# Earlier first operands for a TensorE-bound kernel: other input loads, filler transposes, merged last stores and a new order table

## The chip, the cores and the metric

The kernel runs on one core of one Trainium2 chip. The metric is the device time of one execution in microseconds, the median of several runs. The core has five engines that are named as in the profile: PE (TensorE, matrix products; PEld is its weight load), DVE (VectorE), ACT (ScalarE), POOL (GpSimd) and SP (SyncE, which here only issues transfers). They run at the same time, each through its own instructions in order, and wait for one another by semaphores. Data moves between the off-chip memory and the on-chip memory by DMA transfers, which SP, ACT and POOL issue. POOL's transfers can convert fp32 to fp16 on the way; those of SP and ACT here move bytes as they are.

## The reference

Two stages. The first is an attention between tokens and a small state, for 8 batches and 8 heads, with 512 tokens, 32 state rows and 64 columns per head:

```
scores  = scale * x @ state^T ;  a  = softmax(scores)  ; xread = a  @ state
scores2 = scale * state @ x^T ;  a2 = softmax(scores2) ; sread = a2 @ x
tokens  = concat([xread, sread])          # 8 * 544 = 4352 tokens of 512 columns
```

The second is a mixture of 8 experts over these tokens, with weights P from a gate that is normalised 8 times over rows and columns:

```
P = exp(tokens @ w_gate - max) ; 8 times: P /= row sums, P /= column sums, P *= N / E
out = sum over e of  P[:, e] * ( relu(tokens @ w1[e]) @ w2[e] )      # 512 -> 1024 -> 512
```

## The kernel before

**Two programs behind each other.** The second one, from about 140 us to the end, is a plain loop over experts 1 to 7 and over 9 blocks of tokens (8 blocks of 512, and the 256 `sread` tokens). It is dense on PE: `hidden_ps` (L255) for the first product, seven half-size products per block in `layer2` (L334) for the second, and DVE's scaled additions into `acc` (L348). It ends with `layer2_last`: expert 7 on the 256 `sread` tokens, two rows of 128 tokens, matrix products at L312, scaled additions at L314 and the last stores at L317. Row 0 is one product of 512 columns, row 1 two of 256. Each row is stored in four transfers of 32 partitions, alternately from SP and ACT.

**The first program** does all of the attention, expert 0, the gate and the start of expert 1. Its pieces of work are 736 numbered `ops`, and the text table `PLAN` lists them in the order in which they are issued, with the engine that gets each ("62P" is op 62 on PE). `issue` walks through this table. Each engine works in order, so the table fixes what stands ahead of what on PE, DVE, ACT, POOL and on SP's and ACT's transfer queues. The times beside the ops in the code are the planner's estimates that made the table; they do not act at run time.

**What the start consists of**, with the line by which the profile shows each:

- `state` is loaded by two transfers, from SP and ACT (L441), in pieces of 64 floats, and copied as fp16 to `st_in` (`place`: L419 when ACT copies, L421 when DVE does). PE transposes it in 16 products (`turn`, L492) and ACT or DVE copies the result to `stT` (`keep`).
- `x` of a batch (here x0, x1 and so on) is loaded in two halves of four heads by POOL (L468), with conversion to fp16. For x0 and x1 PE transposes each half in 8 products (`turnX`, L578), and two copies take them to `xT`. From x2 on, SP's transposing transfers do that (L591).
- Half a batch is a unit (u0 and u1 belong to x0, u2 and u3 to x1). Its scores are computed as state by tokens (`score`, L605, tile `psB`); u0 and u1 also as tokens by state (`scoreA`, L684, tile `psA`, with the spread-out copy `stD` of the state, cleared at L504). DVE takes maxima (L640, L688) and differences (L691), ACT exponentials (L652, L656), DVE sums and normalises (L666 to L670), PE transposes back (`turnA`, L709), and a copy makes `aT` (`keepA`).
- Expert 0's `w1` and `w2` come in four halves by POOL (L545, L548). `V` is the state times `w1` (L870), so that the first layer (`hidden_mul`, L897, tile `hps`) is V by `aT`. The second layer is L935. The gate uses `G` (L520), the state times `w_gate`.

Loads that POOL issues stand in one queue with POOL's normalisations (L662, L670). The first products at L897 need both units of x0, and with them PE's dense work begins.

Of the kernel before, what the change touches and what calls it, by code (L numbers as in the profile page):

```python
# [16 lines left out]
6G 0S 1S 2V 7H 44V 3A 33V 32A 34A 8G 56P 36P 35V 55H 37V 10H 45V 57A 42P 58V 9G 38P 40P 43A 59P 4S 39A 41V 5V  # L17
46V 62P 50H 51G 61A 71V 63P 60A 52G 64V 11G 72V 73A 80P 65V 12G 435P 401P 66A 81V 13H 79P 14G 82V 436A 88V
437A 404P 83A 67V 402A 137H 403A 89V 96H 97P 100P 84V 406A 68V 90A 98A 15G 85V 69P 86P 53G 405A 99V 87V 70A
103P 101A 102A 91V 409P 16H 92G 413P 104V 407P 410A 411P 105V 111A 438P 120P 414V 408A 419P 421P 106V 415P  # L20
112V 138S 121V 74V 439A 412A 422V 113V 417P 107A 54G 440A 75G 122V 432P 429P 123V 370V 420A 469P 128A 418A
416A 17G 108V 140P 124A 125V 423P 426P 471A 433P 114A 148V 93S 129V 430P 149V 172H 424P 76S 434A 115V 470A
109G 130V 139S 110V 126G 141V 131A 427P 18G 127V 142V 428V 431A 445P 143V 132V 94P 150A 95V 77P 425A 156P 116G
447P 151V 133V 78V 449P 446A 443P 441P 144A 455P 164V 152G 448A 117S 19H 450V 157V 444A 165V 173S 442A 451P
456A 166A 134S 20G 452A 453P 463P 158V 472P 207H 145V 175P 159V 183V 184V 457P 31G 146G 454A 176V 473A 160A
464P 185A 174S 460P 458P 461P 465A 147V 161V 21G 153S 177V 191P 47P 162G 474A 118P 167V 459A 154P 462A 178V
163V 135P 49A 168G 199V 22H 48V 179A 466P 136A 352P 475P 200V 192V 201A 193V 119V 467P 476A 194V 23G 195A 485P
202V 208S 210P 180V 169S 155A 218V 356P 353A 481P 357V 468A 487P 219V 24G 489P 181G 186V 211V 242H 486A 482A
477P 490V 488A 483P 479P 220A 170P 478A 503P 187G 480A 484V 171A 203G 196V 537P 209S 25H 212V 226P 197G 504A
505A 506P 213V 500P 182V 198V 26G 234V 221V 507A 222V 204S 188S 491P 27G 538A 227V 539A 501P 497P 502A 508A  # L30
492P 235V 243S 228V 244S 214A 229V 511P 215V 236A 523P 230A 498P 494P 216G 245P 495P 515P 512V 499A 277H 231V
524A 493A 517P 246V 253V 223S 496A 247V 521P 516A 237V 254V 519P 509P 522V 518A 248V 513P 232G 189P 520A 255A
205P 510V 224P 514V 540P 28H 278S 261P 249A 190V 269V 29G 225A 270V 262V 531P 534P 206V 238G 250V 532P 256V
358P 271A 535P 217V 541A 533A 233V 542A 312H 279S 263V 272V 536A 354P 280P 528P 543P 529P 525P 288V 289V 251G
555P 264V 281V 265A 282V 239S 257V 526P 359A 266V 544A 530V 556A 545P 355A 547P 549P 273G 553P 527A 546V 571P
313S 290A 548A 283V 605P 550A 554V 296P 267G 606V 304V 572A 305V 240P 573A 557P 284A 607A 558A 551P 297V 552A
568P 360P 258S 241V 285V 30G 291V 306A 559P 562P 574P 298V 252V 315P 299V 286V 569P 576A 268V 323V 563P 575A
274S 300A 560P 570A 292G 316V 361A 561A 581P 564A 307V 565P 362P 324V 317V 301V 325A 302G 566P 363V 582A 326V
579P 587P 583P 287V 314S 588V 591P 567A 580A 639P 608P 584A 592A 347H 303V 331P 577P 348G 641V 640A 610A 609A
339V 293S 589P 585P 275P 332V 259P 578A 327G 586A 260A 590A 294P 340V 308G 333V 341A 593P 309S 318V 319A 334V  # L40
295V 364P 594P 276V 328S 625P 619P 342V 595A 335A 365A 599P 320V 602P 343V 336V 600P 337V 603P 626A 321G 322V
329P 310P 350G 344S 601A 349G 311A 620V 345P 338V 346V 604V 366P 596P 330A 368P 369V 351G 597P 367A 371V 611P
372P 598A 695H 615P 617P 373V 612V 374P 375V 613P 614V 616A 623P 618A 621P 696H 711H 376A 705P 377V 642P 624A
622A 706A 707A 630P 643V 697V 708P 644A 378P 379V 631P 710A 627P 698V 380V 647P 632A 709A 636P 628P 381P 633P
699V 648V 637P 382V 634P 657P 629A 638A 383V 700V 653P 658A 655P 384P 651P 635A 701V 654A 725P 385V 723P 386V
702V 656A 726A 716P 652A 724A 717A 645P 659P 649P 714P 646A 650A 660A 387P 721P 715A 712P 727P 687P 722A 388V
728A 688A 667P 713A 664P 389V 390P 703V 665P 668P 391V 673P 674A 392V 661P 670P 669A 729V 393P 671P 394V 666A
662P 672A 677P 395V 718P 663A 678A 679P 675P 683P 719A 681P 720V 680A 676A 685P 396P 684A 682A 397V 686A 692P
704V 689P 693P 690P 730P 398V 694A 399P 733P 731V 691A 732A 735A 734A 400V
""".split()  # L50
ENGINES = {"P": "PE", "V": "DVE", "A": "ACT", "G": "POOL", "D": "DMA", "S": "SPQ", "H": "HOST"}
NT_ = 2
ETX = 0
POOLB = 1
# [50 lines left out]
def issue(ops):  # L105
    for step in PLAN:
        op = ops[int(step[:-1])]
        assert all(d.end for d in op.after) and ENGINES[step[-1]] in op.on
        for slot in op.takes:
            slot.ring.taken.append(slot)  # L110
            slot.tile = slot.make()
        op.emit(ENGINES[step[-1]])
        op.end = True
    assert all(op.end for op in ops) and len(PLAN) == len(ops)
# [3 lines left out]
def kernel(  # L118
# [9 lines left out]
    nc = tc.nc  # L128
# [170 lines left out]
    def layer2_last():  # L299
# [5 lines left out]
        for row in range(tn // 128):  # L305
# [10 lines left out]
            for i in range(nb):  # L316
                (nc.scalar if i % 2 else nc.sync).dma_start(  # L317
                    out=outs[row * nb + i], in_=acc[ds(i * Ns, Ns), k, :])
# [116 lines left out]
    st_in = spl.tile([128, B, NQ, 2, D], FP16, name="st_in")  # L435
    st_st = spl.tile([128, B, NQ, D], FP32, name="st_st")
    loads = []
    for g in range(2):
        def load(g=g):
            bs = ds(g * B // 2, B // 2)  # L440
            (nc.scalar if g else nc.sync).dma_start(  # L441
                out=st_st[:, bs], in_=state[bs].rearrange("b (q h) n d -> (h n) b q d", q=NQ))

        loads.append(dma((0, 0), 1.0, load, lands=2.7))
        ops[-1].since, ops[-1].hard = 0.5, 1
# [5 lines left out]
    wgd = dma((0, 2), 0.1, lambda: nc.sync.dma_start(  # L451
        out=wg_st, in_=moe_w_gate.rearrange("(kc p) e -> p kc e", p=128)))
    wgc = op((15.0,), {"DVE": (0.15, 0.25)}, lambda _: nc.vector.tensor_copy(out=wgh, in_=wg_st), [wgd])
    wgc.since = 20.0
# [7 lines left out]
    for b in range(B):  # L462
        x_ready.append([])
        part("x%d" % b)
        got = op((0, 1 + 2 * b), {"HOST": (0.0, 0.0)}, lambda _: None, takes=[xn[b]])
        for g in range(2):
            def load(b=b, g=g):
                nc.gpsimd.dma_start(  # L468
                    out=xn[b].tile[:, ds(g * 4, 4), :],
                    in_=x[b, ds(g * 4, 4), :, :].rearrange("h (p sc) d -> p h (sc d)", sc=NSC))  # L470

            x_ready[b].append(dma((0, 1 + 2 * b, g), 1.28 if b else 2.3 - 0.6 * g, load, [got], [], [xn[b]], "POOL"))
            ops[-1].since, ops[-1].hard = 0.7, 1
# [4 lines left out]
    bd = []  # L478
    for g in range(2):
        for s_ in range(2):  # L480
            def place(eng, g=g, s_=s_):
                bs = ds(g * B // 2, B // 2)
                copy(eng, st_in[:, bs, :, s_, :], st_st[:, bs])

            bd.append(op((0, 0, g), {"DVE": (0.50, 0.64)} if s_ else {"ACT": (0.50, 0.65)}, place, loads[g:g + 1] + warmed))
    stT_ready = []
    for g in range(4):
        ps = psum([128, 4, 128], FP16, "stT_ps")

        def turn(_, g=g, ps=ps):  # L490
            for i in range(4):
                nc.tensor.transpose(ps.tile[:, i], st_in[:, 2 * g + i // 2, i % 2].rearrange("p s d -> p (s d)"),  # L492
                                    identh)

        def keep(eng, g=g, ps=ps):
            copy(eng, stT[:, ds(2 * g, 2)].rearrange("p b q c -> p (b q) c"), ps.tile)

        t = op((0, 1, g), {"PE": (0.35, 0.55)}, turn, bd[g // 2 * 2:g // 2 * 2 + 2] + [makeh], [ps])
        stT_ready.append(op((0, 1, g), EVICT16, keep, [t], uses=[ps]))
    ND = (TOK + 1) // 2  # L500
    stD_ready = {}
    if TOK:
        stD = spl.tile([128, ND, NQ, 4, 2, Ns], FP16, name="stD")
        zd = op((0, 0, 0), {"POOL": (0.40, 0.50), "DVE": (0.25, 0.35)}, lambda eng: engines[eng].memset(stD, 0.0))  # L504
        for b in range(ND):
            def spread(eng, s_, b=b):
# [4 lines left out]
                               lambda eng, s_=s_, spread=spread: spread(eng, s_), stT_ready[b // 2:b // 2 + 1] + [zd])  # L511
# [55 lines left out]
    for b in range(B):  # L567
# [4 lines left out]
                  [x_ready[b][0]], [xT])  # L572
        for g in range(2 if b < NT else 0):
# [11 lines left out]
            t = op((due_x(2 * b + g) - 2.0, 0), {"PE": (0.70, 0.88)}, turnX, [x_ready[b][g], makeh], [ps], [xn[b]])  # L585
# [3 lines left out]
        for g in range(0 if b < NT else 2):  # L589
# [5 lines left out]
            xt_ready.append([dma((due_x(2 * b - 2), 0, g), 2.0, turn, [x_ready[b][g], gotT], [], [xn[b], xT], lands=0.8)])  # L595
            ops[-1].moves, ops[-1].xbar = (3.0, 0.8), 1
            ops[-1].on = {"SPQ": (1.4, 4.5)}
        for q in range(NQ):
# [18 lines left out]
            o2 = op((due_x(2 * b + q), 0), {"PE": (0.13, 0.38)}, score, xt_ready[q] + stT_ready,  # L617
# [490 lines left out]
```

## Time and profile before

| | us |
|---|---|
| median of 3 runs | 754.57 (753.24 to 755.26) |
| the profiled execution, its own time | 753.05 |
| its span, first to last instruction | 751.3 |
| PE busy in the span | 734.7 |
| ACT busy, DVE busy | 518.2, 616.3 |
| x0's halves landed (L468) | 6.93 and 8.13 |
| the halves of w1 landed (L545) | 10.9 and 13.4 |
| x1's halves landed (L468) | 14.8 and 16.2 |
| first product of L897 | 18.66 |
| last addition of L314 ends | 747.81 |

Landing times are issue time plus the time to landing that the list of transfers gives (the first half of x0: 1.43 + 5.5). In the profile, a tile's row has the engine, the line, the operation with output and input, the count, and behind it how long the engine sat idle before and for whom it waited. In the table by stretches, each row gives a stretch, and then busy time and instructions of PE, PEld, DVE, ACT and POOL, PE's granted clock as a share of full speed, the mean number of transfers that each of the 16 DMA engines has in hand, and the rate in GB/s, counted in bytes as written at the destination.

### The profile page before, as it was taken

To read this page: it belongs to the slowest core of one execution; us is meant where nothing else is said; L and a number is where in the kernel's file an instruction comes from. 1 tells how busy PE (TensorE), PEld (TensorE's weight loads), DVE (VectorE), ACT (ScalarE), POOL (GpSimd) and SP (SyncE) were. 2 spreads that over 40 slices of the span, in tenths; PEclk is the share of its full clock that TensorE was granted. 3 is DMA by queue.
4 is the path that set the end of the run, shared out by engine and by line. 5 is a ranking of instruction groups with operands and counts; after the bars stand their busy time and mean duration, and the time that the engine had idled before them with its cause. 6 is when DMAs were issued, how large, how long until landed. Compare 5 with 4: busy or idle time off the path is not lost.

```text
span 751.3 us, 16144 instructions
## 1 busy us (share of the span) xinstructions
PE 734.7 (98%) x6517; PEld 501.2 (67%) x6517; DVE 616.3 (82%) x1529; ACT 518.2 (69%) x1014; POOL 70.8 (9%) x81
## 2 busy tenths in 40 slices
PE   4999999999999999999999999999999999999997
PEld 3444445667677777777777677776777777776776
DVE  5999989888888789788887888887897888878875
ACT  6876846798976766666666766667667666676662
POOL 3664310200010000100000000100001000000000
PEclk9999999999999999999999999999999999999999
DMA  9997560600032000600006000330006000002234
GB/s 175 151 133 127 86 92 1 113 2 1 1 66 48 2 1 2 113 1 1 2 4 110 2 1 1 58 56 1 1 2 112 2 1 2 1 29 101 98 113 141
DMA packets 51323, 36.71 MB, mean 49 GB/s; under 512 B 25392, under 2 KB 43824, under 8 KB 51248
## 3 DMA queue, kind: packets, MB, share of 16 engines
q0 software_dynamic: 22272, 20.97, 18.4%
q1 hardware_dynamic: 27744, 14.18, 7.7%
q8 instruction: 51, 0.84, 0.5%
q10 hardware_dynamic: 1232, 0.52, 0.3%
q14 instruction: 24, 0.20, 0.1%
HBM read 42.48 MB, written 8.91 MB: 68 GB/s over the span
## 4 chain that ended last, share of the span: by engine, by line
PE 91%; DVE 3%; DMA 2%; ACT 1%; POOL 1%; issue 0%; SPq 0%; POOLq 0%; ACTq 0%
PE hps L255 28%; PE Bseed L334 20%; PE A L334 14%; PE E L334 13%; PE yps L935 6%; PE v_ps L235 4%; PE hps L897 4%; DMA xT<-x_nat 2%; DMA x_nat<-in_x_dram 1%; DVE acc L348 1%; ACT Hm L275 1%; PE su_ps L758 0%; PE y L312 0%; PE v_ps L870 0%; POOL E L662 0%; ACT V L419 0%
## 5 line engine op out<-in xcount | busy, mean ns | idle before, releaser
L275 ACT ACTIVATE Hm<-hps 128x512 f16<-128x512 f32 (+1 forms) x496 | 265.2, 577 | 128.1 <-PE hps L255 125.3
L255 PE MATMUL hps<-aT,V 128*128 128x512 f16 x880 | 230.1, 379 | 0.0
L334 PEld LDWEIGHTS <-Hm 128*128 128x128 f16 x1888 | 181.4, 98 | 71.2 <-issue 15.8
L348 DVE SCALAR_TENSOR_TENSOR acc<-Bseed,Pmat,acc 128x256 f32<-128x256 f32 x354 | 155.0, 477 | 9.4 <-PE Bseed L334 6.6
L334 PEld LDWEIGHTS <-sm 128*128 128x128 f16 x1416 | 138.2, 98 | 34.1 <-issue 0.4
L334 PE MATMUL A<-w2h,Hm 128*128 128x256 f16 x944 | 123.7, 273 | 0.0
L334 PE MATMUL Bseed<-T,Hm 128*128 128x256 f16 x944 | 123.3, 273 | 0.0
L255 PEld LDWEIGHTS <-V 128*128 128x128 f16 x880 | 86.1, 98 | 51.3
L348 DVE SCALAR_TENSOR_TENSOR acc<-E,Pmat,acc 128x256 f32<-128x256 f32 x236 | 103.1, 476 | 12.5 <-PE E L334 12.5
L281 DVE TENSOR_TENSOR sm<-Hm 128x512 f16<-128x512 f16 (+1 forms) x122 | 50.1, 411 | 64.2 <-ACT Hm L275 64.0
L243 ACT CAST V<-v_ps 128x512 f16<-128x512 f32 x150 | 77.7, 611 | 0.0
L348 DVE SCALAR_TENSOR_TENSOR acc<-A,Pmat,acc 128x256 f32<-128x256 f32 x118 | 51.9, 479 | 17.2 <-PE A L334 16.7
L935 PE MATMUL yps<-w2h,hT 128*128 128x512 f16 x272 | 64.1, 379 | 0.0
L363 ACT COPY Bseed<-A 128x512 f32<-128x512 f32 (+1 forms) x62 | 34.1, 550 | 43.3 <-PE A L334 42.1
L334 PE MATMUL E<-T,sm 128*128 128x256 f16 x472 | 61.7, 273 | 0.0
L334 PE MATMUL E<-w2h,sm 128*128 128x256 f16 x472 | 61.7, 273 | 0.0
L334 PE MATMUL Bseed<-T,sm 128*128 128x256 f16 x472 | 61.5, 272 | 0.0
L282 DVE TENSOR_TENSOR Hm<-Hm 128x512 f16<-128x512 f16 (+1 forms) x122 | 50.2, 412 | 4.2
L284 DVE TENSOR_TENSOR sm<-Hm,sm 128x512 f16<-128x512 f16 (+1 forms) x122 | 50.2, 412 | 4.2
L283 DVE TENSOR_TENSOR sm<-sm,Hm 128x512 f16<-128x512 f16 (+1 forms) x122 | 49.4, 405 | 0.0
L194 POOL DMA_DIRECT2D w1h<-in_moe_w_dram x12 | 8.5, 714 | 397.9 <-PE hps L255 397.4
L935 PEld LDWEIGHTS <-hT 128*128 128x128 f16 x272 | 25.4, 99 | 28.8 <-issue 1.7
(127 smaller groups left out, 609.7 us busy)
## 6 DMA issues: line engine op xcount, KB each, us to landing
w1h<-in_moe_w_dram POOLq DMA_DIRECT2D x16, 512.0 KB, 7.0
w2h<-in_moe_w_dram POOLq DMA_DIRECT2D x16, 512.0 KB, 8.1
out_dram<-acc SPq DMA_DIRECT2D x32, 256.0 KB, 2.6
x_nat<-in_x_dram POOLq DMA_DIRECT2D x16, 256.0 KB, 5.6
st_st<-in_state_dram ACTq DMA_DIRECT2D x1, 256.0 KB, 4.9
st_st<-in_state_dram SPq DMA_DIRECT2D x1, 256.0 KB, 4.3
ETs<-E SPq DMA_TRANSPOSE x16, 3.9
out_dram<-acc SPq DMA_DIRECT2D x4, 64.0 KB, 1.7
```

Of the source, the lines that this page charges most:

```text
L235: nc.tensor.matmul(ps[q][ds(j * Ns, Ns), :], stT[ds(r, 64), bi, q, ds((j ^ q) * Ns, Ns)], w1h[ds(r, 64), 2 * q + j // 2, cols], tile_posit ...
L243: nc.scalar.copy(out=dst, in_=src)
L255: nc.tensor.matmul(out, lhs, rhs, start=(k == 0), stop=(k == len(terms) - 1))
L275: nc.scalar.activation(out=Hm[:, i, j, :tn], in_=hps[:, :tn], func=AF.Relu)
L281: nc.vector.tensor_add(s1, a21, a22)
L282: nc.vector.tensor_sub(a21, a11, a21)
L283: nc.vector.tensor_sub(s2, s1, a11)
L284: nc.vector.tensor_sub(s4, a12, s2)
L334: nc.tensor.matmul(dst[:, c], lhs(j, c), rhs[:, j], start=first and c == 0 and j == 0, stop=(j == NJ - 1), skip_group_check=True)
L348: nc.vector.scalar_tensor_tensor(out=dst, in0=src[:, c], scalar=p[:, k], in1=dst, op0=ALU.mult, op1=ALU.add)
L363: nc.scalar.copy(out=Bb[:, :nk], in_=A[:, :nk])
L935: nc.tensor.matmul(yps.tile, hT[fb].tile[:, ds(tk * 128, 128)], w2h[:, fb, :], start=(fb == 0), stop=(fb == NFB - 1))
```

## The change

- **State in 1 KB rows.** The state is loaded with four state rows of a head (1 KB together) per partition, in two transfers from SP: group 0 (128 KB) first, groups 1 to 3 (384 KB) third. `place` makes both copies of a group in one instruction, one per group; the copy to `stT` puts the columns back in order. A batch's score needs only its own group's copy.
- **Half of x0 as fp32.** x0's first half is loaded by SP and ACT (256 KB of fp32 each, 1 KB rows) into rows of `acc` that are still unused, and DVE and ACT convert one quarter each to `x_nat` (`narrow`). POOL loads one half less.
- **Filler transposes.** `idle` writes transposes of the identity into the tile that the next op is about to fill: 24 before the state's first transposes, 2 before x0's first, 14 and 8 before `turnA` of u0 and u1, 5 before the first product at L897.
- **Last stores.** Three instead of eight: row 0 whole (256 KB, SP), and each half of row 1's columns as soon as it is added (128 KB each, SP and ACT). Each one's memory side is four blocks of 32 rows.
- **Another order table** of 739 ops. Now PE's early order is: state group 0; x0 first half; x1 first half; state group 1; scoreA u0; x0 second half; score u0; state group 3; x1 second half; scoreA u1; state group 2; score u2; V of batch 0, half 0; turnA u0; score u1; V of batch 0, half 1; G; turnA u1; V of batch 1, half 0; then L897. POOL's order is: identity, clearing of `stD` (before on DVE), x1 first half, x0 second half, x1 second half, both halves of w1, x2 first half, w2 first half, x2 second half. ACT makes all four copies to `stT`.
- Numbers of the planner's estimates change, which by themselves do nothing.

```diff
-            for i in range(nb):
-                (nc.scalar if i % 2 else nc.sync).dma_start(
-                    out=outs[row * nb + i], in_=acc[ds(i * Ns, Ns), k, :])
+                (nc.scalar if c else nc.sync).dma_start(
+                    out=outs[ds(row * nb, nb), :, cols], in_=acc[:, k, cols])
...
+IDLE = {34: 24, 59: 2, 72: 14, 89: 8, 416: 5}
...
+    st_in = spl.tile([128, B // 2, 4, 2, D], FP16, name="st_in")
+    st_st = spl.tile([128, B // 2, 4 * D], FP32, name="st_st")
+    st_rows = state.rearrange("b h (k l) d -> (b h k) (l d)", l=4).rearrange("(g p) c -> p g c", p=128)
+    xs = acc[:, ds(0, 2 * XH), :].rearrange("p (g t) d -> p g (t d)", t=2)
...
+    def load_st(a, b):
+        return begin("SPQ", lambda: nc.sync.dma_start(out=st_st[:, a:b], in_=st_rows[:, a:b]), 0.35 * (b - a))
+
+    def load_x(g, k):
+        q = nc.scalar if k else nc.sync
+        return begin("ACT" if k else "SPQ", lambda: q.dma_start(
+            out=xs[:, g, ds(k * 512, 512)].rearrange("p (h c) -> p h c", h=2),
+            in_=x[0, ds(4 * g + 2 * k, 2)].rearrange("h (p sc) d -> p h (sc d)", sc=NSC)), 0.68)
+
+    loads = load_st(0, 1)
+    xs_in = [[load_x(g, k) for k in range(2)] for g in range(XH)]
+    loads += load_st(1, B // 2) * 3
...
+            copy(eng, st_in[:, g], st_st[:, g].rearrange("p (l d) -> p l d", d=D).unsqueeze(2)
+                 .broadcast_to((128, 4, 2, D)))
...
+            copy(eng, stT[:, ds(2 * g, 2)].rearrange("p b q (m l) -> p (b q m) l", l=4), ps.tile.rearrange("p (l m) -> p m l", l=4))
...
+    def idle(t, n):
+        if not n:
+            return
+        t = t.rearrange({2: "p a -> p a", 3: "p a b -> p (a b)", 4: "p a b c -> p (a b c)"}[len(t.shape)])[:, :128]
+        for _ in range(n):
+            if t.dtype == FP16:
+                nc.tensor.transpose(t, identh, identh)
+            else:
+                nc.tensor.matmul(t, identh, identh, start=True, stop=True, skip_group_check=True)
```

## The prediction

> **What bounds the kernel now.** I read the page first, then PE's waits, then PE's instructions in order of time, then two tables by stretches, for the start and for the end.
>
> ```profile
> PE 734.7 (98%) x6517; PEld 501.2 (67%) x6517; DVE 616.3 (82%) x1529; ACT 518.2 (69%) x1014; POOL 70.8 (9%) x81
> ...
> PE 91%; DVE 3%; DMA 2%; ACT 1%; POOL 1%; issue 0%; SPq 0%; POOLq 0%; ACTq 0%
> ```
>
> PE is busy 98% and carries 91% of the chain that ended last. So only three things can change the time: PE's idle time, its speed, and what lies behind its last product.
>
> ```profile
> PE xT_ps L578 <- DMA x_nat<-in_x_dram: 8.1, 3, 7.0
> PE psB L605 <- DMA xT<-x_nat: 2.2, 3, 0.9
> PE psB L605 <- ACT E L652: 0.6, 1, 0.6
> PE psA L684 <- ACT xT L419: 0.6, 1, 0.6
> ```
>
> PE waits 7.0 us at the very start for x0, and briefly afterwards. Its instructions in order of time (start, length, count):
>
> ```profile
> 6.98 1.04 PE L578 MATMUL xT_ps<-identh,x_nat 128*128 128x128 f16 x8 [6.98 <-DMA x_nat<-in_x_dram]
> 7.81 1.91 PE L492 MATMUL stT_ps<-identh,st_in 128*128 128x128 f16 x16
> 9.52 0.85 PE L578 MATMUL xT_ps<-identh,x_nat 128*128 128x128 f16 x8
> 14.84 0.62 PE L578 MATMUL xT_ps<-identh,x_nat 128*128 128x128 f16 x8 [0.37 <-DMA x_nat<-in_x_dram]
> 18.66 2.65 PE L897 MATMUL hps<-aT,V 128*128 128x512 f16 x8
> 21.69 1.90 PE L897 MATMUL hps<-aT,V 128*128 128x512 f16 x8
> ```
>
> Two things show here. Dense work begins at 18.66. And PE runs at two speeds: 16 transposes take 1.71 us from start to start at 7.81 (107 ns each), but those at 14.84 about 57 ns; the first eight products of L897 take 2.65 us, the next eight 1.90, of which the last 0.07 to 0.17 overlaps what follows. The table by stretches has the granted clock for the second case (PE is the first engine after the stretch; then PEld, DVE, ACT, POOL, clock, DMA, GB/s):
>
> ```profile
> 10.00:20.00 10.00, 7.15 (x98) 3.77 (x96) 9.38 (x22) 8.71 (x19) 1.04 (x1) 0.84 1.35 199
> ...
> 17.00:18.00 1.00, 0.96 (x8) 0.69 (x8) 0.91 (x2) 1.00 (x5) 0.00 (x0) 0.50 1.50 213
> 18.00:19.00 1.00, 0.93 (x12) 0.33 (x10) 0.81 (x4) 1.00 (x4) 0.04 (x1) 0.50 1.27 196
> 19.00:20.00 1.00, 1.00 (x4) 0.41 (x3) 0.97 (x2) 0.87 (x3) 1.00 (x1) 0.50 1.24 204
> ```
>
> From 10 to 20 us DVE is 94% busy and ACT 87%: their work for u0 and u1 sets when L897 starts. The half clock then meets its first products. (At 7 to 10 us the clock column says 1.00 though the pace is half; there I go by the pace.) From 18.66 on, PE lacks only about 2.7 us (0.76 between 30 and 40 us, 1.38 between 50 and 60, 0.6 elsewhere up to 740). The end:
>
> ```profile
> 745.00:746.00 1.00, 1.00 (x9) 0.70 (x8) 0.42 (x1) 0.00 (x0) 0.00 (x0) 1.00 1.04 377
> ...
> 747.50:748.00 0.50, 0.00 (x0) 0.00 (x0) 0.32 (x1) 0.00 (x0) 0.00 (x0) 1.00 0.97 250
> 749.50:750.00 0.50, 0.00 (x0) 0.00 (x0) 0.00 (x0) 0.00 (x0) 0.00 (x0) 1.00 0.53 135
> ```
>
> The last addition ends at 747.81; then only stores are left, until 751.3.
>
> **Step 1: the loads and the start of dense work.** The old order's DVE chain runs from 10.67 (first maximum of u0) to 17.57 (second product of L670); then turnA, its copy, and L897 at 18.66. For the new order I follow the queues.
>
> POOL clears `stD` before its first load. POOL's clearing of a quarter of those bytes took 0.20, DVE's of all 0.27; I take 0.45 (0.2 to 0.8). The first load is then issued at 1.43 + 0.45 = 1.9. It is x1's first half now, and x0's took 5.5 us beside 512 KB of state in 256-byte pieces; so it lands at 7.4. There is now twice as much beside it (1 MB), but in 1 KB rows. The bounds are 6.4 and 9.9: stores in 2 KB rows moved 377 GB/s where the state moved some 180 to 270, and the load queued third took 7.8 us. The spacing of x halves was 1.2 (6.93 to 8.13), so x0's second half lands at 8.6, x1's second at 9.9; each half of w1 took 2.6, so 12.5 and 15.1.
>
> State group 0 and x0's first half come from SP and ACT. 256 KB took 4.3 to 4.9 us for loads, 2.6 for stores. By either they have landed by about 5, before 7.4, so converting them (0.6 each, the row of the state's copies) is hidden behind the wait for x1. That wait is what takes the place of the old 7.0: on PE, x1's transposes stand ahead of scoreA u0. After 7.4: x1's transposes 0.62, state group 1 about 0.35, scoreA u0 0.41, x0's second half 0.62, the first of its two copies on ACT at 9.5.
>
> From there ACT has no free time until the end of turnA u1's copy: two xT copies 1.07, stT 0.53, expA 0.52, expB 0.78, two stT 1.07, the copy of u2's scores 0.58, xT 0.53, expA 0.53, two V 1.05, aT 0.5, two V 1.05, aT 0.6, together 8.8, with gaps 8.9. So 9.5 + 8.9 = 18.4. DVE starts the maximum of u0 at 9.3 and needs 7.9 to u1's product (three maxima and two differences 3.4, two sums 1.86, two products 1.22, flip 0.70, xT 0.42, small ones 0.3), which ends at 17.2, so it is not last. Dense work at 18.4 instead of 18.66: **-0.25 us**; by the bounds of the loads and the other engine's chain 17.2 to 20.5.
>
> G is now ahead of it. At 42.19 it cost PE 0.64 (next start 42.83) of dense time: **-0.6**. The other early products are the same in both orders.
>
> **Step 2: the clock.** If PE is at full speed at the first L897, 2.65 becomes about 1.73: **-0.9**. The fillers (24 from 1.4 to 4.0 at 107 ns; 14 and 8 ahead of turnA, at 57 ns 0.8 and 0.45) lie in waits for x, DVE and ACT; without these they would cost PE up to 1.5, but there DVE and ACT are last. The 5 before L897 (0.3) lie beside turnA u1's copy (0.6). Between 13 and 17 us PE now has some 0.6 to 0.7 of its time filled; before, 0.46 to 0.68 was followed by the half clock. That is a thin margin.
>
> Here a page speaks against it. The Trainium skill, page "TensorE: Matmul & The Clock Gate", section "Part 4: PE-mode transpose", says that transposes do not count as PE activity for the clock. By it the -0.9 would be 0. The trace disagrees: between 6.98 and 10.29 PE did only transposes, 32 of them, and by 10.3 the pace was full (L605 eight in 0.30, against 0.41 at 18.17).
>
> **Step 3: the rest of the order.** I keep the 2.7 us of waits (0 to 5). Those for transposed x hang on POOL's loads, and POOL's queue is still mixed with normalisations. x2's second half now stands behind a half of w2, which costs it some 2.6, against a scoring that is needed only at 32. State copies with scattered columns stay on ACT at 0.53 to 0.69. Planner figures, wg's place and the missing dependences on other groups: 0.
>
> **Step 4: the stores.** Before: row 1's last of two stores per queue is issued at 748.3 behind the other, lands 2.0 later at 750.3, and the span ends 1.0 after. With one per queue, issued at 747.85, this gains 0.45, less 0.05 for twice the bytes: -0.4, if a store still runs on all 16 DMA engines. This is the lower bound. But each new store names memory as four blocks of 32 rows. All transfers on this page that reach 377 GB/s have at least 32 rows as the outer count on both sides, and what is dealt out can only follow the counts that an instruction carries. If four blocks go to four engines, they move 4/16 of 377 to 417, 94 to 104 GB/s. All three stores, 524 kB, then need 5.0 to 5.6 us from the first byte at about 747.1, to 752.1 to 752.7 instead of 749.75: +2.4 to +3.0. No row shows an outer count of four; the rows with both counts at 32 or more are the only support for the lower bound and do not cover it. I take **+2.5** and keep both ends.
>
> The Trainium skill, page "DMA: Bandwidth & Descriptors", section "Why a DMA increments its semaphore by 16 and not by 1", gives the largest number up to 16 that divides both outer counts as the number of engines, here four. By it the sum would be the one below, by its opposite the first rival. No run here shows it.
>
> **Sum.** -0.25 - 0.6 - 0.9 + 2.5 = +0.75 us on the profiled execution: 753.05 becomes 753.8 (span 752.05; the 1.75 around it unchanged). The median shown is 1.52 above that execution, so I carry the difference over: 754.57 + 0.75 = **755.3**.
>
> **Rivals.**
> - *Stores on all engines*: -0.4 for +2.5, sum -2.15, **752.4**. For it: 64 KB stores run at up to 371 GB/s though small. Chance 0.22.
> - *Late software loads (slower)*: the 1 MB of SP and ACT holds back POOL's loads, and PE is stuck behind x1's first half while x0 lies ready. From 7.4 on each us is a us for dense work. At the bound, 9.9, this adds 2.5: **757.8**. For it: the old loads took 5.5 to 14.8 us by their place in the queue. Against: 1 KB rows are moved faster. Chance 0.17.
> - *A better order*: half of the 2.7 us of waits goes, and dense work begins at 17.4: -2.3 more, **753.0**. Chance 0.13.
> - *The clock stays low*: +0.9, **756.2**. Chance 0.10.
>
> The forecast has 0.38, with its own range 753.3 to 757.3 (start and later waits). About 0.3%, 2.3 us, is what a measurement of this kernel can tell from no change. Faster by more than that: 0.38 x 0.12 + 0.22 x 0.5 + 0.13 x 0.4 = 0.21. Slower: 0.38 x 0.22 + 0.17 x 0.85 + 0.10 x 0.35 = 0.26. Within: 0.53. The range 751.0 to 758.2 takes in all five cases and 1.4 below the first rival; some 0.18 is left out.
>
> **What would show it.** Right: x1's first half lands near 7.4; L897 starts near 18.4, its first eight products in about 1.8 at clock 1.00; G before it; DMA at about 100 GB/s after 748, the end about 6 us after the last addition. Wrong: an end 3.1 us after the last addition (stores on all engines); L897 after 19.5; the clock at 0.50 in its first products; waits of PE between 20 and 140 far from 2.7.

## The result, and the profile after

The changed kernel takes 772.36 us (median of 4 runs, 771.06 to 774.4) against 754.56 for the kernel before in the same series: 1.024 times as long, with a 95% interval of 1.0212 to 1.0268. Forecast were 755.3 us and a range of 751.0 to 758.2; the time lies 14 us above that range. The profiled execution took 771.66 us, with a span of 769.8.

The page of the kernel after, first part and shares of the chain that ended last:

```profile
PE 743.6 (97%) x6570; PEld 507.4 (66%) x6570; DVE 617.0 (80%) x1525; ACT 519.8 (68%) x1018; POOL 73.1 (9%) x82
...
PE 87%; DMA 5%; DVE 5%; ACT 1%; issue 1%; POOL 1%; SPq 0%; POOLq 0%; ACTq 0%
```

PE carries 87% of the chain instead of 91%, DMA 5% instead of 2%. PE is also 8.9 us longer busy; the 53 fillers are a part of that, and for the rest its speed has to be read too. What PE waited for (total us, times, longest):

```profile
PE psB L627 <- DMA xT<-x_nat: 7.1, 3, 3.6
PE su_ps L780 <- DMA ETs<-E: 3.5, 2, 2.8
PE xT_ps L600 <- DMA x_nat<-in_x_dram: 1.5, 1, 1.5
```

The 7.0 us at the start are gone; in their place, PE waits 7.1 us for transposed x (2.2 before) and 3.5 for transposed exponentials. PE's instructions in order of time say where:

```profile
8.37 1.03 PE L600 MATMUL xT_ps<-identh,x_nat 128*128 128x128 f16 x8 [1.46 <-DMA x_nat<-in_x_dram]
...
19.62 1.46 PE L919 MATMUL hps<-aT,V 128*128 128x512 f16 x6
...
34.76 0.41 PE L627 MATMUL psB<-xT,stT 64*32 64x256 f16 x8 [3.59 <-DMA xT<-x_nat]
35.11 1.89 PE L957 MATMUL yps<-w2h,hT 128*128 128x512 f16 x4
...
55.20 0.30 PE L627 MATMUL psB<-xT,stT 64*32 64x256 f16 x8 [2.74 <-DMA xT<-x_nat]
...
83.59 0.69 PE L780 MATMUL su_ps<-ETs,x_nat 128*64 128x32 f16 x32 [2.83 <-DMA ETs<-E]
```

Dense work (L919, which was L897) starts at 19.62, not at 18.4, and there it runs at full speed: six products in 1.46. The long waits come later, at 31.17, 52.5 and 80.8. Behind the first, four products of 512 columns take 1.68 from start to start, twice their usual 0.86. The table by stretches has the clock for it:

```profile
30.00:40.00 10.00, 6.41 (x60) 2.52 (x55) 4.58 (x12) 4.89 (x13) 3.12 (x2) 0.67 0.91 122
...
50.00:60.00 10.00, 7.26 (x84) 3.25 (x82) 7.73 (x18) 6.71 (x16) 4.76 (x5) 1.00 0.94 156
...
80.00:90.00 10.00, 7.17 (x91) 3.49 (x83) 6.72 (x15) 4.09 (x10) 1.67 (x3) 0.83 0.70 112
```

The first of these rows had PE at 9.24 and clock 1.00 before. Such rows from 20 to 150 us give 11.06 us without work on PE, where the kernel before has 2.52. In rows of 1 us the clock is 0.50 from 34 to 40 and from 85 to 88, with a part of a row on either side; that is 5.4 and 3.4 us of work at half speed, and half of it, 4.4 us, is lost. The end:

```profile
762.00:763.00 1.00, 0.00 (x0) 0.00 (x0) 0.00 (x0) 0.00 (x0) 0.00 (x0) 1.00 0.13 29
...
765.00:766.00 1.00, 0.00 (x0) 0.00 (x0) 0.00 (x0) 0.00 (x0) 0.00 (x0) 0.50 0.27 98
```

After the last addition, at 761.08, the stores run at 95 to 98 GB/s with 0.27 of a transfer per DMA engine, where the kernel before had 250 with 0.97.

**The account.** From the first product of `layer2_last` to the end of the span it was 7.6 us, now 12.9: +5.3. That product starts at 756.92 instead of 743.66: +13.3. Of this the later start of dense work is +0.95, G ahead of it -0.6 (it was inside before), the clock in the first products -0.9, waits from 20 us on +8.5, half speed behind them +4.4: together 12.35. The remaining 0.9 is not assigned.

### The profile page after: what moved, and what is told of

Its sections match the earlier page's. It is cut to its first block, busy times and chain, and to the rows that moved or that the text cites. A ratio compares the mean times of both kernels' runs of the same rounds, so it can differ in the third digit from the quotient of the medians.

```text
span 769.8 us, 16252 instructions
## 1 busy us (share of the span) xinstructions
PE 743.6 (97%) x6570; PEld 507.4 (66%) x6570; DVE 617.0 (80%) x1525; ACT 519.8 (68%) x1018; POOL 73.1 (9%) x82
## 4 chain that ended last, share of the span: by engine, by line
PE 87%; DMA 5%; DVE 5%; ACT 1%; issue 1%; POOL 1%; SPq 0%; POOLq 0%; ACTq 0%
PE hps L258 27%; PE Bseed L336 19%; PE A L336 14%; PE E L336 13%; PE yps L957 5%; PE v_ps L238 4%; PE hps L919 3%; DMA xT<-x_nat 3%; DMA x_nat<-in_x_dram 1%; DMA ETs<-E 1%; DVE acc L350 1%; ACT Hm L278 1%; PE y L315 0%; DVE eA L650 0%; DVE nmB L662 0%
## 5 line engine op out<-in xcount | busy, mean ns | idle before, releaser
L957 PE MATMUL yps<-w2h,hT 128*128 128x512 f16 x272 | 68.2, 392 | 0.1
```

The source lines that it names most:

```text
L957: nc.tensor.matmul(yps.tile, hT[fb].tile[:, ds(tk * 128, 128)], w2h[:, fb, :], start=(fb == 0), stop=(fb == NFB - 1))
```

## The experiments

All of them compute the whole reference. Ratios are to the kernel before, timed on the same chip in the same series. "Old stores" are the eight stores of the kernel before.

**The stores alone.** E1 is the kernel before with the change's store lines; E2 the kernel after with the old ones.

```diff
-            for i in range(nb):
-                (nc.scalar if i % 2 else nc.sync).dma_start(
-                    out=outs[row * nb + i], in_=acc[ds(i * Ns, Ns), k, :])
+                (nc.scalar if c else nc.sync).dma_start(
+                    out=outs[ds(row * nb, nb), :, cols], in_=acc[:, k, cols])
```

> The kernel before with only the three merged stores at its end. Theory 'four engines' (a store whose memory side counts four blocks outermost moves on 4 of the 16 DMA engines): the stretch from the start of the last products (L312) to the end grows from 7.5 us to about 12.7, as in the changed kernel, with some 100 GB/s and a DMA share near 0.25 after the last addition, and the time grows by about 5.2 us (0.7%). Rival 'late issue' (the end grew only because the stores were held up by what stands ahead of them in the changed kernel): no growth, about -0.4 us.

> The changed kernel with the old eight stores. If the end is a loss of its own, it takes back 5.2 us: about 767 us, still 1.6% slower than before, and the end is again some 7.5 us from the first of the last products. If the stores are not the cause, it stays at 772.

E1: 758.25, ratio 1.0059 (1.0042 to 1.0076), 4.4 us. E2: 766.02, 1.0163 (1.0143 to 1.0184), 12.3 us, so that going back to the old stores gains some 6. E8 halves the number of blocks once more, in the kernel before:

```diff
-            for i in range(nb):
-                (nc.scalar if i % 2 else nc.sync).dma_start(
-                    out=outs[row * nb + i], in_=acc[ds(i * Ns, Ns), k, :])
+            for i in range(nb // 2):
+                (nc.scalar if i else nc.sync).dma_start(
+                    out=outs[ds(row * nb + 2 * i, 2)], in_=acc[ds(2 * i * Ns, 2 * Ns), k, :])
```

> The kernel before with its last rows stored in four transfers whose memory side counts two blocks of 32 rows outermost (128 KB each, SP and ACT in turn). Theory 'the outer count sets the number of engines': two of sixteen, some 49 GB/s, 524 kB in 10.7 us instead of 5.4, so the time is about 5 us above that with three stores of four blocks, near 763 us, at a DMA share of about 0.13. Rival 'merged blocks are slow as such, at one rate': near 758 us and 100 GB/s, as with four.

It takes 765.36, 1.0151 (1.0128 to 1.0175). One row of the table by stretches each, E1 and then E8:

```profile
751.00:752.00 1.00, 0.00 (x0) 0.00 (x0) 0.00 (x0) 0.00 (x0) 0.00 (x0) 0.50 0.26 98
```

```profile
755.00:756.00 1.00, 0.00 (x0) 0.00 (x0) 0.00 (x0) 0.00 (x0) 0.00 (x0) 0.50 0.13 51
```

The two last columns are a quarter and 98 GB/s with four blocks, an eighth and 51 with two: 4 and 2 of the 16 engines. In the old shape (32 rows outermost) the last stores have 0.97 to 1.00 and move 250 to 258, in the rows of the kernel before from 747.5 to 748 and from 749 to 749.5. Its 377 GB/s belong to the 256 KB stores ahead of them. Stores explain some 5 us of 18; the order and the loads are left with 12.

**Loads or order.** E3 has the change's loads and code, old stores, and the order of the kernel before in the new numbering (new ops where their neighbours are).

```diff
-IDLE = {34: 24, 59: 2, 72: 14, 89: 8, 416: 5}
+IDLE = {59: 24, 72: 14, 89: 8, 412: 5}
```

> The changed kernel with the old eight stores and with the old order table, carried over op by op: the new state and x0 loads, the narrowing copies and the fillers (24, 14, 8, 5, at the ops with the same role) stay. Theory 'the order is at fault' (13 us of the loss lie in what PE waits for under the new order): near the time before, 752 to 757 us, waits of PE between 20 and 140 us of 2 to 4 us. Rival 'the loads are at fault' (1 MB through SP and ACT delays POOL's loads and everything behind them, whatever the order): 763 to 768 us, with waits for transposed x as in the changed kernel.

754.69, 1.001 (0.9995 to 1.0024). The loss is gone: it is the order table's.

**One wait at a time.** The first long wait is that of `score` of u5 for x2's second half. In the kernel after, its transposing transfer stands on SP behind two of `ETs` and is issued at 26.64; POOL issues both halves of x3 at 26.28. It takes 8.1 us, where the kernel before has 4.5, with POOL's two loads issued apart, at 24.67 and 28.43. The place on SP is no difference: the kernel before has two transfers of `ETs` ahead of it as well. SP in order of time, after and before:

```profile
20.79 5.73 SPq L764 DMA_TRANSPOSE ETs<-E  x2
26.64 1.24 SPq L613 DMA_TRANSPOSE xT<-x_nat  x1
```

```profile
20.55 5.37 SPq L742 DMA_TRANSPOSE ETs<-E  x2
25.96 1.32 SPq L591 DMA_TRANSPOSE xT<-x_nat  x1
```

Three edits, each on E2, by op numbers: E4 moves the transfer (142) ahead of those of `ETs`; E5 moves the loads of x3 (18, 19) behind a normalisation of POOL; E6 moves `score` of u5 (159) behind six further pieces of PE's work.

```diff
-133V 79S 118V 127A 96S 142S
+133V 142S 79S 118V 127A 96S
...
-18G 152V 144V ... 142S 19G ... 146V 119G
+152V 144V ... 142S ... 146V 119G 18G 19G
...
-135V 159P 130V ... 452P 448P
+135V 130V ... 452P 159P 167V 168V 160V 161V 448P
```

> The changed kernel with the old eight stores, and on SP the transposing transfer of x2's second half ahead of both transposing transfers of E of u0 and u1 instead of behind them. Theory 'queue on SP': it is issued at about 22.1, when x2's second half has landed, instead of 26.64, clear of x3's loads, so that PE's wait of 3.6 us near 31 to 35 us and the half clock behind it (2.6 us) go: about 761 us. Theory 'beside the loads' (it takes 8.1 us because x3's two loads run beside it): the same here, since it moves ahead of these. Rival 'planned too tightly everywhere': the waits only move to the next transfers, and the time stays within 2 us of 767.

> The changed kernel with the old eight stores (766.0 us), and POOL's two loads of x3 behind the normalisation of u2's E instead of ahead of it, some 3 us later. Theory 'beside the loads': the transposing transfer of x2's second half, still issued near 26.6, takes 4.5 to 5.5 us instead of 8.1, as in the kernel before, where one load of x ran beside it and not two; PE's wait near 31 to 35 us shrinks from 3.8 to about 1, the time falls by some 3 to 5 us, less what x3's own later arrival costs further on. Rival 'queue on SP alone': it still takes about 8 us, and the time does not fall.

> The changed kernel with the old eight stores (766.0 us), and on PE the score of u5, which waits for that transfer, behind six more ops of dense work (3.4 us) instead of ahead of them; DVE's and ACT's ops of u5 follow it. Theory 'PE asks too early': the wait of 3.8 us and the half clock behind it (2.6 us) go, and some of it comes back as later work of u5: 760 to 762 us. Rival 'the chain behind is the bound' (the attention of the later units arrives late anyway, and PE only waits elsewhere): within 2 us of 766.

E4: 762.22, 1.0107 (1.0089 to 1.0126). E5: 762.86, 1.0124 (1.0107 to 1.0142). E6: 763.65, 1.0127 (1.0105 to 1.0149). The transfer's row in the list of transfers (median us to landing), after and E5:

```profile
xT<-x_nat SPq DMA_TRANSPOSE x1, 8.1
```

```profile
xT<-x_nat SPq DMA_TRANSPOSE x1, 3.0
```

So each of the three takes away the first wait, as expected, and by the ratios gives 4.2, 2.9 and 2.7 us; E6 is 1.7 us slower than the end of its range. The later waits stay (in E4 3.23 at 47.3 and 2.77 at 75.9, in E6 2.80 and 2.48). The same loads paired in the kernel before are E14:

```diff
-16A 17G 108V 140P ... 427P 18G
+16A 17G 18G 108V 140P ... 427P
```

> The kernel before with one op moved: POOL's second load of x3 directly behind the first, at about 25.5 us, instead of behind two normalisations at 28.4. Theory 'pairs of loads': the transposing transfer of x2's second half, issued at 25.96, takes 6.5 to 8 us instead of 4.5 and lands after PE has reached the score of u5 at 32.0; PE waits up to 2 us there, and the time grows by 1 to 4 us. Rival: that transfer keeps its 4.5 to 5 us and the time stays within 1 us of before.

755.01, 1.0016 (1.0005 to 1.0027). The transfer takes 6.6 instead of 4.5, so that the loads beside it do slow it. But it lands at 33.6, and PE comes to the score at 33.67 and does not wait; in this execution it came 1.6 us later than in the kernel before, whose first eight products took 2.65 and not 3.56. After 20 us PE waits for transposed x only 0.6 in all, against 2.2 before, so the growth of 1.2 us is not explained by that transfer. So two loads together are one part of the wait in the new table (E5), and that PE asks earlier there is another (E6).

**Several at a time.** E10 makes all three edits. E13 pulls apart every pair of x loads that the new table puts together (18, 19, 24, 25, 30, 31, each behind a later normalisation of POOL). E15 is E13 with the edit of E4.

> The changed kernel with the old eight stores (766.0 us) and all three edits of the order: x2's second transposing transfer ahead of those of E, POOL's loads of x3 three microseconds later, the score of u5 behind six ops of dense work. Theory 'one wait, and the same kind of wait further on': the edits cure the same wait near 31 to 35 us, so their gains (3.8, 3.2, 2.4 us) do not add up; 760 to 763 us, with the waits near 50 us (transposed x) and near 80 us (transposed E) still there. Rival 'they add': about 757 us.

> The changed kernel with the old eight stores (766.0 us), with POOL's loads moved so that no two loads of x stand back to back beside a transposing transfer that PE waits for: x3's two behind the normalisations of u2 and u3, x5's first behind that of u6, x5's second behind that of u8, x7's two behind that of u11. Theory 'pairs of loads beside the transposing transfers': all three waits shrink, PE's waits between 30 and 90 us fall from about 10 us to 4 to 6, and with them the half clock behind: 757 to 761 us. Rival 'DVE's and POOL's chain is late anyway' (normalisations on POOL wait for DVE up to 4 us at a time, and loads stand behind them): the waits come back under other names, 762 to 764 us, no better than with one pair moved (762.9).

> As the run with all pairs apart, and x2's second transposing transfer ahead of those of E on SP. If the waits have one cause each and this one was already cured by moving x3's loads: equal to that run within 1.5 us. If the place in SP's queue is a loss of its own: 2 us or more faster.

E10: 763.23, 1.0134 (1.0109 to 1.0158). E13: 761.98, 1.0119 (1.0097 to 1.0141). E15: 764.03, 1.0144 (1.0113 to 1.0175). The gains do not add. E13 came out at the edge of what its rival said, and E15 is neither equal to it nor faster: 1.9 us slower by the ratios, with intervals that overlap. E13 shows why. In PE's order of time its waits for transposed x come back in other places (1.46 before 40.23, 1.21 before 61.49, 1.70 before 69.12, and the longest), and the chain has the steps ahead of the longest:

```profile
87.14 0.30 PE L628 MATMUL psB<-xT,stT 64*32 64x256 f16 x8 [2.85 <-DMA xT<-x_nat]
```

```profile
79.14 4.42 DMA x_nat<-in_x_dram
...
83.58 3.51 DMA xT<-x_nat
```

And POOL in order of time:

```profile
78.15 1.05 POOL L693 TENSOR_TENSOR a<-eA,rA 128x512 f16<-128x512 f32 x1 [3.11 <-DVE rA L690]
79.14 0.82 POOL L489 DMA_DIRECT2D x_nat<-in_x_dram  x1
```

The load stands on POOL behind a normalisation that waits 3.11 us for DVE; DVE's sums need exponentials, and these a score of PE. PE, ACT, DVE, POOL, load, transposing transfer and again PE form a loop; the chain shows its steps from DVE on, the rest is read from the program. The edit that took this load away from its neighbour is what put it behind that normalisation.

**Which part of the table.** Three splices with old stores: E16 takes the new table up to the first product of L919 (94 of 739 ops) and the old sequence for the rest; E17 the old one up to there, then the new; E18 the new one up to `score` of u8 (266 ops, about 55 us), then the old.

```diff
-L = new
+L = head(new, "H mul b0 fb3") + rest(old)   # E16
+L = head(old, "H mul b0 fb1") + rest(new)   # E17
+L = head(new, "score u8") + rest(old)       # E18
```

> New order table up to and with the first product of expert 0's first layer (about 19.6 us, 94 of 739 ops, all the early loads among them), from there the old order's sequence for all that is left; eight stores as before. Theory A, the new table's sequence after 20 us makes TensorE wait: the total is near the old order's, 754 to 757. Rival B, the start of the new table (x2's second half behind a half of w2, landing 2.2 us later) sets off the later waits: 762 or more. Rival C, each part brings its own share: 758 to 761.

> The other way round: the old order up to its first product of expert 0's first layer (about 19 us, 89 ops), and from there the new table's sequence for all that is left; eight stores as before. Theory A: the waits stay, 763 to 767. Rival B: the waits go, 754 to 757. Rival C: 758 to 761.

> New table up to and with the score of unit 8 (about 55 us, 266 ops), then the old order's sequence; eight stores as before. It keeps the first two long waits of the new table (3.6 and 2.7 us, and about 3 us of half clock behind the first) and drops the later ones (1.3 and 2.8, with about 1.5 us of half clock). Theory A with each stretch paying for itself: about 754.5 + 7 to 9 = 761 to 764. If the later waits follow from the state the earlier stretch leaves behind (data already late at 55 us), the total stays at 765 to 767. If the early waits are worked off by a better order behind them, 756 to 759.

E16: 754.24, 1.0007 (0.9998 to 1.0016). E17: 761.98, 1.0115 (1.0099 to 1.0132). E18: 760.54, 1.0105 (1.0077 to 1.0133). In E16 theory A holds: the start of the new table costs nothing, x2's late second half included; what follows 20 us does. E17 and E18 agree in kind, but they stay 1.0 and 0.5 us below theory A's ranges. PE's waits for transposed x in E16 and then in E18 (a kernel with old stores is one line longer, so L627 is L628 there):

```profile
PE psB L628 <- DMA xT<-x_nat: 2.0, 3, 0.9
```

```profile
PE psB L628 <- DMA xT<-x_nat: 6.0, 3, 3.7
```

E16 has the loads, the fillers and the stages up to 20 us of the changed kernel, and still the old waits. The transposing transfer of u5 is issued on SP at nearly the same time, and PE's score comes later (E16, first SP and then PE in order of time):

```profile
26.10 1.51 SPq L614 DMA_TRANSPOSE xT<-x_nat  x1
```

```profile
33.51 0.30 PE L628 MATMUL psB<-xT,stT 64*32 64x256 f16 x8
```

There POOL's x3 loads are issued apart, at 24.70 and 29.07; the transfer takes 5.7 and lands at 31.8, 1.7 us ahead of the score. In the kernel after PE is ready for the score at 31.17, and the data lands at 34.7. By the ratios, the stretch from 20 to 55 us costs 7.4 us (E18 less E16) and the rest 4.4 (E2 less E18), each to within 2 to 3 us. E17 loses only 8.7 with the whole of it behind the old head, so a part depends on how the table is entered.

**The fillers.** E9 is E2, and E7 is E3, without them (`IDLE = {}`). E11 puts 64 ahead of x0's transposes in the kernel before, E12 6 and 10 more ahead of x1's.

```diff
+IDLE = {56: 64}                    # E11
+IDLE = {56: 64, 97: 6, 100: 10}    # E12
```

> The changed kernel with the old eight stores and no filler transposes (with them 766.0 us). Theory: under the new order the fillers lie in real waits of PE and only keep the clock up, so that without them the first products of L920 run at half clock again: 0.5 to 1.5 us slower, about 767. Rival 'fillers only cost', as the 1 us under the old order suggests: about 765.

> The kernel with the new loads under the old order (754.7 us with fillers), without any filler transposes. Theory 'clock bought with delay': in the run with fillers the 14 ahead of the turnA of u0 ran at half clock and put it back by 0.7 us (17.75 instead of 17.04), so that dense work began 0.8 us later but at full clock (eight products 1.89 instead of 2.65). Without fillers dense work begins near 18.7 at half clock: the same time within 1 us. Rival 'fillers gain': 1 to 2 us slower without them. Rival 'fillers only cost': 1 to 2 us faster without them.

> The kernel before, old loads, old order, old stores, with 64 filler transposes ahead of PE's first transposes, which wait for x0 until 6.98 us. About 32 run at 107 ns, the rest at 57 ns, from 1.35 to about 6.4. Theory 'a warm start': the 32 transposes up to 10.3 us take 1.9 instead of 3.3, DVE's chain of u0 starts about 1 us earlier, and so does dense work; if the clock then falls again before it, as before, the gain is 1 us: about 753. If it stays up, 2 us: 752. Rival 'the chain is bound elsewhere' (x1's load at 16.2 stands ahead of the turnA of u0 on PE): no gain beyond 0.3 us from the earlier start.

> As the run with 64 fillers first, and 6 and 10 more ahead of the transposes of x1's halves, which wait for their loads at 14.84 and 16.22. Theory: these lie in true waits and delay nothing; PE's share in use before dense work rises and the clock stays at full speed into the first products of L897 (eight in 1.9 us, not 2.65): 0.9 us less than without them, about 752. Rival: the clock falls all the same; equal to the run without them.

E9: 766.69, 1.0174 (1.0151 to 1.0197), its six first products in 2.74, against 1.46 in the kernel after. E7: 753.64, 0.9996 (0.9987 to 1.0004), not slower than E3, though its first eight products take 2.75, against 1.89 in E3. E11: 754.77, 1.0012 (1.0000 to 1.0024), without the gain that its theory expected: the fillers run past the landing of x0, the clock falls at 14.1 all the same, and the first eight take 2.81. E12: 753.09, 1.0000 (0.9986 to 1.0013). There the clock falls at 13.7 as well, but it is back at 17.1, and the first products run at full speed:

```profile
18.74 1.89 PE L899 MATMUL hps<-aT,V 128*128 128x512 f16 x8 [0.22 <-ACT aT L421]
```

That is 0.76 less than the kernel before needs for them (2.65), and yet the total is the same: waits of 0.7 for `w2h` at 27.63, and 0.70 to 1.24 for transposed data further on, take it back.

One run has the fillers and the half clock all the same. E15 has the fillers of the kernel after, and its clock is 0.50 from 19.2 to 22.6:

```profile
20.98 2.26 PE L920 MATMUL hps<-aT,V 128*128 128x512 f16 x6
```

Of the 13 profiled executions with fillers in the waits just ahead of dense work, 12 have the first products at full speed; of the 7 without, none has.

## Why the prediction was wrong, by its own steps

- **Step 3 failed**: "I keep the 2.7 us of waits (0 to 5)". They became 11.06, and behind them came 4.4 us lost at half speed, for which the sum had no term: its step on the clock ends with the first products. E16 to E18 put both into the sequence after 20 us. I had followed the queues of the new table up to the first dense product only, and carried a number of the old table over for the 720 us behind it. What differs at the first long wait can be read from the table without any run: POOL issues both loads of x3 together, and PE has the score of u5 three pieces of dense work earlier (40 products of 512 columns of the two layers ahead of it, where the kernel before has 50). The range of 0 to 5 rested on no row of the new order. The step's specific worry, x2's second half behind a half of w2, was rightly put at nothing: it landed at 22.1 instead of 19.9, and E16 has it so, too.
- **Step 1** had the wrong sign: 19.6 for 18.4, +0.95 for -0.25, inside its bounds. The eleven profiled executions that start with the new loads and the new table lie between 18.9 and 21.0. x1's first half landed at 8.32, not at 7.4, the second half of w1 at 17.3, not at 15.1, and the first transposes ran at half speed (1.03 against the 0.62 assumed), so that the first copy of x0's second half on ACT began at 11.14, not at 9.5; from there to dense work it took 8.5, near the 8.9 of the sum. G moved ahead as said.
- **Step 2** was right: clock 1.00 at the first products, -0.9 for them. E9, E7 and E12 show that the fillers do it, and E15 that the margin is as thin as step 2 said. Here the Trainium skill, page "TensorE: Matmul & The Clock Gate", section "Part 4: PE-mode transpose", which has transposes not count for the clock, does not agree with the runs: with only more transposes E12 needs 1.89 for the eight products, E11 2.81. But the gain stays in the stretch; none of the comparisons (E9 to E2, E7 to E3, E12 to before) makes the total faster by what can be told apart.
- **Step 4** had the mechanism and missed the size. Four blocks run on four engines, two on two (E1, E8); the rate is the 94 to 104 GB/s foreseen. I had the first byte at 747.1, while the last products still run. In the kernel after SP issues its two stores at 759.63 for 1.37 us and ACT its one at 761.11 for 1.15, where a store took 0.32 to 0.43 to issue before; only 25 to 29 GB/s flow until 763, and the 524 kB end near 768.5. That makes +4.4 in E1 and about +6 from the kernel after to E2, for +2.5.
- **The rivals**: stores on all engines is refuted by E1 and E8; late software loads came to a third of its price (0.9 us of 2.5) and decided nothing; the clock did not stay low; the order turned out worse, not better. That the new order is much worse was no rival at all, though the sentence on what would show the prediction wrong did name the waits between 20 and 140 us.

What stays open: which places of the sequence after 20 us make up the loss. Single ones were found for some 3 to 4 us (E4, E5, E6), and no run with any of that sequence past the first dense products has a median below 760. No version was measurably faster than the kernel before: the best are E7 at 0.9996 and E12 at 1.0000.

## What to carry to other kernels

A new order written out by hand is to be followed on every queue for as long as it differs, not up to the place that the change is about: for each late-arriving operand, set issue, neighbours on the same path and the time at which the consumer asks side by side. A wait of some 3 us on the engine that bounds the kernel can cost more than one and a half times its length (3.59 and 2.7 behind it, 2.83 and 1.7), because the clock falls with it; whether it falls also depends on where the wait lies (2.74 and nothing behind it). And a store merged to save issues has to keep an outer count on the memory side that all DMA engines can share.

## What the runs showed of the hardware that was not expected

- The granted clock falls within a wait or behind it, and comes back late: PE stopped at 31.17, the clock was 0.50 from 33.4 on, and it stayed there for 5.4 us of work after the wait had ended at 34.76. After the wait from 80.8 to 83.6 it fell at 84.6, when PE was at work again, and stayed low until 88.0. After the wait of 2.74 before 55.20 it did not fall; in E2 it did, behind the same wait of 2.78 before 54.26 (low from 55.6 to 59.0).
- In the kernel after, the two low stretches last 6.8 and 3.4 us, and in all 20 profiled executions every low stretch ahead of the last products lasts 3.4 or 6.8. So the clock seems to be set anew in steps of 3.4 us. Counted from the fall at 33.4, PE was busy 1.2 us in the step before that fall and 1.0 us in the step before the fall at 84.6; the wait before 55.20 is shared by two steps with 2.0 and 2.1 us of work. The steps are an estimate from these lengths.
- A transposing transfer of half a batch took 3.0 us with no x load next to it (E5, E13), 5.0 beside a load of w2 (E4), 4.5 to 5.7 with single ones about it (before, E16) and 6.5 to 8.3 with two of 256 KB issued close to it (E14, E6, after, E2).
- DMA engines in use for a store followed the outer count: with 32 rows, four blocks and two blocks outermost the last stores had 0.97 to 1.00, 0.26 to 0.27 and 0.13 of a transfer per engine, and moved 250 to 258, 98 and 51 GB/s.
